# A block-sparse attention and MLP kernel: another order of a batch's tiles, and other sources for the first tiles' V

## The chip, the core and the metric

The kernel runs on one core of a Trainium2 chip. Its engines run side by side, each through its own list of instructions: PE (matmul), PEld (its weight loads), DVE and ACT (vector and scalar work), POOL (GpSimd), and SP, which here only issues DMAs. POOL issues DMAs too, through a queue of its own. The metric is the time of one execution in microseconds (us), lower is better.

## The reference

Attention with a mask of blocks, then a two-layer MLP on its output, in fp32.

```python
batch, n_heads, seq, head_dim = (4, 8, 768, 64)      # blocks of 32: 24 block rows, 3 sampled blocks a row
mask = np.abs(blk_i - blk_j) <= window               # window = 1
mask = mask | (blk_i == 0) | (blk_j == 0) | (blk_i == n_blocks - 1) | (blk_j == n_blocks - 1)
mask[qb * block:(qb + 1) * block, kb * block:(kb + 1) * block] = True   # for kb in sampled_blocks[qb]
scores = np.where(mask, scale * q @ k.T, -1e9)
attn = softmax(scores)
x = (attn @ v)                                       # 3072 tokens x 512
h = np.maximum(x @ w_in, 0.0)                        # 512 x 2048
out = h * h @ w_out                                  # 2048 x 512
```

So each query block sees its neighbours, the first and the last block (static, the same for all), and three sampled ones. The first and the last block row of a batch see all keys.

## The kernel before

**Tiles and chunks.** A tile is 128 rows (four query blocks) of a batch with all eight heads; a batch has NT = 6. Three tiles (UC) make a chunk of 384 tokens, so there are NCH = 8 chunks, two of a batch. A tile is done in two Halves of four heads: scores s (L374), maxima m (L385), exps p (L423), turn pt (L437) and its copies pT (L446), values pv (L459), norm rec and x (L474 to L479). The global rows, first and last block of a batch, are done by four Wholes, a head pair each: g (L546), exps pg (L562), turn ptg (L584), copies pTg (L592, L594), pvg (L604), norm. They fill the first rows of tile 0 and the last rows of tile 5. A Whole reads its V from vn, a batch's V rows (L222, two halves of 780 KB, one buffer for each half); a Half reads V, which is put together from static blocks (L203 and copies L209), neighbours (the window, L304, or copies L217 out of vn) and sampled blocks (L317, 12 loads a tile). Keys of a tile stand in KG: static (L284), sampled (copies L263 by POOL out of kn in batch 0, DMAs L276 later); neighbours are read from kn itself.

**The MLP.** For a chunk, moe() turns x (xt, L773, with the casts xh and xl, L776 and L777), makes ph for each of 16 slices of 128 hidden units (L788), r and g out of it (L792 to L806), and po (L816 in chunk 0, L826 later). In matmuls, values are split in a high and a low part. The weights come as 64-bit floats (craw, L692, on POOL's queue); cut() makes fp32 of them in chunk 0: two ACT passes (L708, L710) and two DVE passes (L719, L720); high and low parts follow (L726, L727, L752, L755).

**The order of work.** It is written out by hand: each engine runs in the order in which the program records. A Stream steps through units and resumes each after lags set by tables (LAG_0 and so on). Chunk 0's units run before any MLP work; that stretch is called the startup here. While moe(c) runs, the units of chunk c + 1 are recorded between its steps. Before the change a batch's Wholes stand in the even chunks, so batch 0's are in the startup, and the order of tiles is 0 to 5. In the loop of the startup, copies of static blocks and windows and cuts are put in at set steps (FIXED_0, MOVES_0, CUT_0). On PSUM a pool of five banks goes round among s, pt, g, xt and ph.

Of the kernel before, what the change touches and what calls it, by code (L numbers as in the profile page):

```python
# [2 lines left out]

# [66 lines left out]

STEP_0 = 5
STEP_1, FIRST_1 = 12, 0
LAG_1 = {**LAG, "v": 10, "x": 3, "t": 6, "v0": 5, "n": 0}
LAG_0 = {"s": 2, "x": 2, "t": 3, "c": 2, "v0": 2, "n": 2}
# [4 lines left out]
MOVES_0 = 22


FIXED_0 = 7
ON_ACT = 12
KEYS_N = 2
# [12 lines left out]
def tile_block_sparse_attention_moe(ctx: ExitStack, tc, kd, knd, qd, qgd, vd, vnd, samp, const, wcat, out):  # L97
# [112 lines left out]

    def copy_window(k, i, j, n, copy):

        b, t = order[k]
        blk = centre(NJ * t + j) - 1 + n
        assert 0 < blk < NBLK - 1
        r = blk % NJ * BLK
        copy(V[k][1][(1 + n) * BLK : (2 + n) * BLK, i, j], st["vn", b, i][r : r + BLK, blk // NJ])  # L217

    def load_vn(b, hf, eng=nc.sync, own=None):

        vn = (own or rot).tile([P, NT, HW // 2], F32, tag="vn", name=f"vn{b}_{hf}", bufs=1)
        eng.dma_start(vn.rearrange("p t c -> p (t c)"), vnd[b, hf])  # L222
# [30 lines left out]
    def copy_keys(b, t, own=None):  # L253

        vals = sampled(t, 0, POOL)
        kg = keys_of(b, t, own)
        for u in range(2):
            if t < UC:
                static_keys(b, t, u, nc.gpsimd.tensor_copy)
            kn = st["kn", b, u]  # L260
            for j in range(NJ):
                for r in range(NRAND):
                    nc.gpsimd.tensor_copy(  # L263
                        kg[:, j, 2 + r, 2 * u : 2 * u + 2].unsqueeze(1), kn[:, bass.ds(vals[NRAND * j + r], 1)]
                    )
                yield
# [13 lines left out]
    def static_keys(b, t, u, copy=nc.scalar.copy):  # L280

        src = st["kn", b, u][:, 0 : NBLK : NBLK - 1].rearrange("p i a c -> p i (a c)").unsqueeze(1)
        dst = st["kg", b, t][:, :, 0:2, 2 * u : 2 * u + 2].rearrange("p j i a c -> p j i (a c)")
        copy(dst, src.broadcast_to(list(dst.shape)))  # L284
# [480 lines left out]
    def turn(c):  # L765

        xh = pool["x"].tile([P, NCC, TOK], F32R, tag="xh", name=f"xh{c}", bufs=1)
        xl = pool["x"].tile([P, NCC, TOK], F32R, tag="xl", name=f"xl{c}", bufs=1)
        for i in range(UC):
            x = X.pop(order[c * UC + i])  # L770
            pt = bank(f"xt{c}_{i}")
            for cc in range(NCC):
                nc.tensor.transpose(pt[:, cc * P : (cc + 1) * P], x[:, cc * P : (cc + 1) * P], ident)  # L773
            p3 = pt.rearrange("p (c q) -> p c q", c=NCC)
            at = slice(i * P, (i + 1) * P)
            nc.scalar.copy(xh[:, :, at], p3)  # L776
            nc.vector.tensor_tensor(xl[:, :, at], p3, xh[:, :, at], op=ALU.subtract)  # L777
        xs[c] = (xh, xl)

# [115 lines left out]
    for k in range(2):  # L895
        deque(copy_keys(0, k), 0)
    for _ in range(AHEAD):
        cut_next()
    for k in range(1, UC):
        if k == 1:  # L900
            for f, *at in windows[k, 0]:
                f(*at, nc.gpsimd.tensor_copy)
            deque(copy_keys(0, 2, begin), 0)
# [102 lines left out]
```

## Time and profile before

| | us |
|---|---|
| median of 3 runs | 759.31 (759.08 to 762.59) |
| the profiled execution | 760.55, span 758.8 |
| PE busy in the span | 732.4 (97%) |
| ACT, POOL, DVE busy | 539.7, 502.3, 499.8 |
| first xt (x of chunk 0 is complete) | 57.3 |
| DMA, mean | 128 GB/s, 283 in the first 19 us |

The span is that of the profiled execution from its first to its last instruction; the time beside it includes what lies around. The rows of the trace are read as start, duration, engine, line, operation, output and inputs, count; in brackets stands how long the engine was idle before and what ended that. ph, po and s overlap their neighbours on PE, so that their price is the distance from start to start.

### The profile page before, as it was taken

To read this page: it belongs to the slowest core of one execution; us is meant where nothing else is said; L and a number is where in the kernel's file an instruction comes from. 1 tells how busy PE (TensorE), PEld (TensorE's weight loads), DVE (VectorE), ACT (ScalarE), POOL (GpSimd) and SP (SyncE) were. 2 spreads that over 40 slices of the span, in tenths; PEclk is the share of its full clock that TensorE was granted. 3 is DMA by queue.
4 is the path that set the end of the run, shared out by engine and by line. 5 is a ranking of instruction groups with operands and counts; after the bars stand their busy time and mean duration, and the time that the engine had idled before them with its cause. 6 is when DMAs were issued, how large, how long until landed. Compare 5 with 4: busy or idle time off the path is not lost.

```text
span 758.8 us, 26292 instructions
## 1 busy us (share of the span) xinstructions
PE 732.4 (97%) x9832; PEld 612.3 (81%) x9832; DVE 499.8 (66%) x987; ACT 539.7 (71%) x1193; POOL 502.3 (66%) x636
## 2 busy tenths in 40 slices
PE   4879999999999999999999999999999999999997
PEld 2656776668888888888888888887888888888986
DVE  5785785658785756667777575666868666645452
ACT  5896877798876876789786767679876776733222
POOL 6963844227776675757767567666876575777885
PEclk9799999999999999999999999999999999999999
DMA  8776799544543536544434344655344352201001
GB/s 283 224 215 172 228 264 344 130 117 131 140 114 93 146 86 176 153 109 128 113 105 106 101 126 109 221 120 140 79 124 118 75 143 64 51 1 44 1 1 41
DMA packets 92290, 97.45 MB, mean 128 GB/s; under 512 B 14787, under 2 KB 79428, under 8 KB 92164
## 3 DMA queue, kind: packets, MB, share of 16 engines
q1 hardware_dynamic: 86036, 72.41, 37.1%
q0 software_dynamic: 5696, 22.58, 9.2%
q8 instruction: 78, 1.28, 0.7%
q10 hardware_dynamic: 432, 0.79, 0.3%
q14 instruction: 48, 0.39, 0.2%
HBM read 89.43 MB, written 6.29 MB: 126 GB/s over the span
## 4 chain that ended last, share of the span: by engine, by line
PE 85%; ACT 5%; DMA 4%; DVE 4%; issue 1%; SPq 1%; ACTq 0%; POOL 0%; DVEq 0%; POOLq 0%
PE ph L788 33%; PE po L826 30%; PE s L374 7%; PE pv L459 5%; PE po L816 4%; PE g L546 2%; PE pvg L604 2%; DMA V<-in_v_dram 2%; DMA KG<-in_k_dram 1%; PE xt L773 1%; PE pt L437 1%; DVE xl L777 1%; ACT V L209 1%; DMA kn<-in_kn_dram 1%; SPq L317 1%
## 5 line engine op out<-in xcount | busy, mean ns | idle before, releaser
L413 ACT ACTIVATE pm<-p 32x256 f32<-32x256 f32 x576 | 239.2, 415 | 13.2 <-DVE p L391 4.8
L788 PE MATMUL ph<-xh,wi 128*128 128x384 f32 x832 | 237.8, 347 | 0.0
L826 PE MATMUL po<-wo,gh 128*128 128x512 f32 x672 | 213.8, 399 | 0.0
L755 POOL TENSOR_TENSOR wi<-W,wi 128x512 fp32r<-128x512 f32 x104 | 142.3, 1368 | 68.4 <-DVE wi L754 35.2
L806 POOL TENSOR_TENSOR gl<-gf,gh 128x384 fp32r<-128x384 f32 x112 | 117.4, 1048 | 93.0 <-DVE gf L804 80.6
L755 POOL TENSOR_TENSOR wo<-WO,wo 128x512 fp32r<-128x512 f32 x112 | 145.9, 1302 | 49.5 <-DVE wo L754 48.5
L792 ACT ACTIVATE r<-ph 128x384 f32<-128x384 f32 x128 | 63.0, 492 | 161.3 <-PE ph L788 156.1
L804 DVE SCALAR_TENSOR_TENSOR gf<-ph,r 128x384 f32<-128x384 f32 x112 | 62.3, 556 | 150.3 <-ACT r L792 136.4
L788 PEld LDWEIGHTS ph<-xh,wi 128*128 128x128 f32 x832 | 150.4, 188 | 13.4 <-issue 7.4
L826 PEld LDWEIGHTS po<-wo,gh 128*128 128x128 f32 x672 | 123.5, 188 | 23.0 <-issue 2.8
L788 PE MATMUL ph<-xl,wi 128*128 128x384 f32 x416 | 141.4, 340 | 0.0
L826 PE MATMUL po<-wo,gl 128*128 128x512 f32 x336 | 133.2, 396 | 0.0
L754 DVE CAST wo<-WO 128x512 fp32r<-128x512 f32 x112 | 84.4, 753 | 0.0
L788 PEld LDWEIGHTS ph<-xl,wi 128*128 128x128 f32 x416 | 78.2, 188 | 6.9 <-issue 2.9
L826 PEld LDWEIGHTS po<-wo,gl 128*128 128x128 f32 x336 | 63.1, 188 | 15.7 <-POOL gl L806 1.0
L385 DVE TENSOR_REDUCE m<-s 128x2 f32<-128x512 f32 x96 | 61.6, 683 | 11.2 <-PE s L374 10.9
L799 ACT ACTIVATE gh<-r 128x384 fp32r<-128x384 f32 x112 | 59.0, 526 | 9.3 <-ACT r L792 0.4
L459 PEld LDWEIGHTS pv<-V,pT 128*32 128x32 f32 x3072 | 47.7, 110 | 19.8 <-issue 9.5
L459 PE MATMUL pv<-V,pT 128*32 128x65 f32 x3072 | 56.2, 223 | 5.0 <-ACT pT L446 4.8
L788 PE MATMUL ph<-xh,WI 128*128 128x384 f32 x192 | 54.4, 344 | 0.8 <-ACT xh L776 0.8
L374 PE MATMUL s<-KG,q 64*32 64x160 f32 x1536 | 51.2, 305 | 1.4 <-issue 1.0
L418 DVE STREAM_TRANSPOSE pT<-pm 128x1024 f32<-128x1024 f32 x36 | 44.6, 1239 | 4.9 <-ACT pm L413 4.7
(85 smaller groups left out, 933.0 us busy)
## 6 DMA issues: line engine op xcount, KB each, us to landing
craw<-in_w_dram POOLq DMA_DIRECT2D x32, 512.0 KB, 5.9
V<-in_v_dram SPq DMA_DIRECT2D x504, 32.5 KB, 1.8
KG<-in_k_dram SPq DMA_DIRECT2D x216, 64.0 KB, 2.0
V<-in_v_dram SPq DMA_DIRECT2D x28, 390.0 KB, 4.5
q<-in_q_dram SPq DMA_DIRECT2D x24, 256.0 KB, 3.0
out_dram<-ot SPq DMA_DIRECT2D x21, 256.0 KB, 2.5
V<-in_v_dram SPq DMA_DIRECT2D x16, 292.5 KB, 4.2
vn<-in_vn_dram SPq DMA_DIRECT2D x5, 780.0 KB, 6.4
```

The costliest lines, as they stand in the source:

```text
L374: nc.tensor.matmul(self.sb[e][j * BLK : (j + 1) * BLK, i * NSLOT + a : i * NSLOT + z], q[r, j, pr, :], k, start=True, stop=True,)
L385: nc.vector.tensor_reduce(m[:, e], self.sb[e].rearrange("p (i c) -> p i c", i=2), axis=AX, op=ALU.max)
L413: nc.scalar.activation(p[a * BLK : (a + 1) * BLK, j], x[j * BLK : (j + 1) * BLK, :, a], AF.Exp, scale=SCALE)
L459: nc.tensor.matmul(po[j * BLK : (j + 1) * BLK, h * VW : (h + 1) * VW], self.pT[:, j, 2 * e + i, c], v[:, self.u, j, hv : hv + VW], start=( ...
L754: nc.vector.tensor_copy(w[:, 0], src)
L755: nc.gpsimd.tensor_tensor(w[:, 1], src, w[:, 0], op=ALU.subtract)
L788: nc.tensor.matmul(ph[:, :TOK], w, x, start=(i == 0), stop=(i == len(steps) - 1))
L792: nc.scalar.activation(r, ph[:, :TOK], AF.Relu)
L799: nc.scalar.activation(gh, r, AF.Square)
L804: nc.vector.scalar_tensor_tensor(gf, ph[:, :TOK], 0.0, r, op0=ALU.max, op1=ALU.mult)
L806: nc.gpsimd.tensor_tensor(gl, gf, gh, op=ALU.subtract)
L826: nc.tensor.matmul(acc[c][u], g[:, at], w[:, k], start=(f == 0 and i == 0), stop=(f == NF - 1 and i == 2))
```

## The change

A batch's tiles are taken in the order 1 to 5, 0. Chunk 2b then holds tiles 1 to 3 of batch b, and chunk 2b + 1 tiles 4, 5, 0, and the Wholes run beside that second chunk: those of batch 0 while moe(0) runs, those of batch b while moe(2b) runs. V's windows of the second and third tile come from memory by POOL's queue (copy_window goes; there were 48 such copies, 12 on POOL, 18 on DVE, 18 on ACT by the table); vn of batch 0 is loaded later, on SP. Keys' static copies of the first three tiles go from POOL to ACT, V's static copies from ACT to DVE. x of chunk 0 is turned tile by tile in the startup and not in one go at moe(0)'s start. Lags and steps of the tables are set anew (EARLY 23 to 21, STEP_0 5 to 4, LAG_0, LAG_1, WO_LOW 3 to 2). The counts of matmuls stay.

```diff
-CUT_0 = (30, 5)
+CUT_0 = (13, 7)
-order = [(b, t) for b in range(B) for t in range(NT)]
+order = [(b, t % NT) for b in range(B) for t in range(1, NT + 1)]
 def copy_keys(b, t, own=None):
-            if t < UC:
-                static_keys(b, t, u, nc.gpsimd.tensor_copy)
+            if k < UC:
+                static_keys(b, t, u)
...
 def units(c):
-        wholes = [] if c % 2 else [Whole(c // 2, pr) for pr in range(NPAIR)]
+        wholes = [] if c % 2 == 0 else [Whole(c // 2, pr) for pr in range(NPAIR)]
...
         if c == 1:
-            return [(i * STEP_1 + FIRST_1, u) for i, u in enumerate(halves)]
+            both = [(i * STEP_1 + FIRST_1, u) for i, u in enumerate(halves)]
+            both += [(i * STEP_1 + FIRST_1 + G_1, u) for i, u in enumerate(wholes)]
+            return sorted(both, key=lambda x: x[0])
...
 def moe(c):
-        if c < NCH:
+        if 0 < c < NCH:
             turn(c)
...
 # the startup
     load_keys(0, 0, nc.gpsimd)
-    load_whole(0)
-    load_q(0, 0)
+    load_keys(0, 1, nc.gpsimd)
+    load_q(*order[0])
+    load_window(0, 0)
     load_static(0, 0)
-    load_vn(0, 0, nc.gpsimd)
-    load_keys(0, 1, nc.gpsimd)
-    load_vn(0, 1, nc.gpsimd, begin)
-    load_window(0, 0)
-    load_q(0, 1)
     load_sampled(0, 0, nc.sync, SP)
-    load_sampled(1, 0, nc.sync, SP)
-    load_q(0, 2, own=begin)
-    load_sampled(2, 1, nc.sync, SP)
-    windows = {
-        (k, u): [(copy_window, k, u, j, n) for j in range(NJ) for n in range(3)] for k in range(1, UC) for u in range(2)
-    }
...
+    load_q(*order[1], nc.gpsimd)
+    load_q(*order[2], nc.gpsimd, "x", 5)
+    others = [
+        lambda: load_window(1, 0, nc.gpsimd),
+        lambda: load_sampled(1, 0, nc.sync, SP),
+        lambda: load_window(2, 1, nc.gpsimd),
+        lambda: load_sampled(2, 1, nc.sync, SP),
+        lambda: load_whole(0),
+        lambda: load_vn(0, 0),
+    ]
+    for i, _ in enumerate(chain(copy_keys(*order[0]), copy_keys(*order[1]), copy_keys(*order[2], begin))):
+        for at, f in chain(zip(LOADS_0, [cut_next] * AHEAD), zip(OTHERS_0, others)):
+            if at == i:
+                f()
     fixed = [(copy_static, k, i) for k in range(UC) for i in range(2)]
...
+    turns = [(2 * STEP_0 * i + STEP_0 + TURN_0[0], i) for i in range(UC)]
     for at, u in units(0):
+        while turns and turns[0][0] < at:
+            turn_at, i = turns.pop(0)
+            work.add(turn_at, 0, lambda i=i: turn_tile(0, i, TURN_0[1]))
         work.add(at, 0, lambda u=u: u.run(side, LAG_0))
...
         if now >= FIXED_0 and fixed:
             f, *at = fixed.pop(0)
-            f(*at, nc.scalar.copy)
-        if now >= MOVES_0 and moves:
-            f, *at = moves.pop(0)
             f(*at, nc.vector.tensor_copy)
```

Three places in the order. The first is SP at the start: the names are q (queries by batch and tile), V0 and V1 (the first tile's V), V10 and V11, V20 and V21 (the second's and third's); idx are the sampled numbers. Before:

```order
L170 DMA QG_77<-in_qg_dram 128x512
L242 DMA q0_0_129<-in_q_dram 128x512
L203 DMA V0_78<-in_v_dram 64x260 x2
L304 DMA V1_79<-in_v_dram 96x260 x2
L304 DMA V1_79<-in_v_dram 96x3x260 [waits DMAHW0_49]
L304 DMA V1_79<-in_v_dram 96x3x260 [waits DMAHW1_49]
L242 DMA q0_1_143<-in_q_dram 128x512 [waits DMAHW2_49]
L231 TENSOR_LOAD idx_116 [waits DVE_49]
L317 DMA V0_78<-in_v_dram 32x2x260 [waits DMAHW3_49]
L317 DMA V0_78<-in_v_dram 32x2x260 [waits DMAHW4_49]
L317 DMA V1_79<-in_v_dram 32x2x260 [waits DMAHW5_49]
```

and now:

```order
L238 DMA q0_1_132<-in_q_dram 128x512
L302 DMA V1_79<-in_v_dram 96x4x260 x2
L207 DMA V0_78<-in_v_dram 64x260 x2
L227 TENSOR_LOAD idx_115 [waits DVE_49]
L315 DMA V0_78<-in_v_dram 32x2x260
L315 DMA V0_78<-in_v_dram 32x2x260 [waits DMAHW0_49]
L315 DMA V1_79<-in_v_dram 32x2x260 [waits DMAHW1_49]
L315 DMA V0_78<-in_v_dram 32x2x260 [waits DMAHW2_49]
```

QG and the second and third q are gone from here, and the sampled loads start right behind the first tile's window; each waits for a semaphore in turn, eight in all. POOL's queue at the start, where kn are the keys of the two head halves and the copies are sampled keys; before:

```order
L175 DMA kn_0_126<-in_kn_dram 128x1536
L222 DMA vn_0_133<-in_vn_dram 128x1560
masks.py:199 AFFINE_SELECT ident<-ident 128x128
L175 DMA kn_1_135<-in_kn_dram 128x1536
L222 DMA vn_1_137<-in_vn_dram 128x1560
L231 TENSOR_LOAD idx
L284 COPY KG_93<-kn_0_126 128x4x2x64
L263 COPY KG_93<-kn_0_126 128x64
```

and now:

```order
L179 DMA kn_0_128<-in_kn_dram 128x1536
L179 DMA kn_1_130<-in_kn_dram 128x1536
masks.py:199 AFFINE_SELECT ident<-ident 128x128
L238 DMA q_2_175<-in_q_dram 128x512
L238 DMA q_3_177<-in_q_dram 128x512
L227 TENSOR_LOAD idx
L260 COPY KG_93<-kn_0_128 128x64
```

The queue has both kn and two q where vn stood; weights (craw) and the four windows are issued between the key copies that follow. The second place is ACT at the start of moe(0), from gp0_0 to r0_1 (the numbers are chunk and slice; ct, WO and W are weights being cut; p are exps). Before:

```order
L792 ACTIVATE r0_0_1570<-ph0_0_1518 128x384
L795 ACTIVATE gp0_0_1572<-r0_0_1570 128x384
L708 ACTIVATE ct4_1574<-craw4_0_982 128x512
L710 ACTIVATE craw4_0_982<-craw4_0_982,below_75 128x512
L752 CAST wi0_2_1581<-W12_81 128x512
L423 ACTIVATE p0_3_0_1564<-s0_3_0_0_1523,m0_3_0_1561 128x256 x2
L423 ACTIVATE p0_3_0_1564<-s0_3_0_1_1524,m0_3_0_1561 128x256 x2
L792 ACTIVATE r0_1_1601<-ph0_1_1584 128x384
```

and now:

```order
L800 ACTIVATE r0_0_1279<-ph0_0_1226 128x384
L803 ACTIVATE gp0_0_1281<-r0_0_1279 128x384
L710 ACTIVATE WO0_95<-craw0_1_358 128x512
L712 ACTIVATE craw0_1_358<-craw0_1_358,below_75 128x512
L754 CAST wi0_2_1297<-W12_81 128x512
L710 ACTIVATE WO1_96<-craw1_1_724 128x512
L712 ACTIVATE craw1_1_724<-craw1_1_724,below_75 128x512
L710 ACTIVATE ct4_1306<-craw4_0_932 128x512
L712 ACTIVATE craw4_0_932<-craw4_0_932,below_75 128x512
L423 ACTIVATE p0_4_0_1295<-s0_4_0_0_1241,m0_4_0_1292 128x256 x2
L423 ACTIVATE p0_4_0_1295<-s0_4_0_1_1242,m0_4_0_1292 128x256 x2
L800 ACTIVATE r0_1_1333<-ph0_1_1313 128x384
```

Two more cuts (WO0, WO1) stand between. The third place is SP at the switch from batch 1 to 2. Before:

```order
L317 DMA V1_79<-in_v_dram 32x260 [waits DMAHW0_49]
L175 DMA kn2_0_5572<-in_kn_dram 128x1536 [waits DMASW7_49,DMAHW1_49,DMASW0_49,PE_49]
L170 DMA QG_77<-in_qg_dram 128x512 [waits DMAHW2_49,DMASW0_49]
L222 DMA vn2_0_5575<-in_vn_dram 128x1560 [waits DMAHW3_49]
L304 DMA V1_79<-in_v_dram 96x3x260 [waits DMAHW4_49,PE_49]
L304 DMA V1_79<-in_v_dram 96x260 [waits DMAHW5_49,PE_49]
L231 TENSOR_LOAD idx_116
```

and now:

```order
L315 DMA V1_79<-in_v_dram 32x260 [waits DMAHW0_49]
L179 DMA kn2_0_5461<-in_kn_dram 128x1536 [waits DMASW3_49,DMAHW1_49,DMASW0_49,PE_49]
L174 DMA QG_77<-in_qg_dram 128x512 [waits DMAHW2_49,DMASW4_49]
L218 DMA vn2_0_5464<-in_vn_dram 128x1560 [waits DMAHW3_49,PE_49]
L302 DMA V1_79<-in_v_dram 96x260 [waits DMAHW4_49]
L302 DMA V1_79<-in_v_dram 96x3x260 [waits DMAHW5_49]
L227 TENSOR_LOAD idx_115
```

vn2_0 now waits for PE too (the last pvg of batch 1), and the loads of V, kn, q and KG follow it on the queue.

More of the change, by code (lines that the diff above doesn't have):

```diff
@@ L2 @@
 from contextlib import ExitStack, suppress
+from itertools import chain
 import numpy as np
@@ L64 @@
 STEP = PIECES // (2 * UC)
-EARLY = 23
+EARLY = 21
 LAST = 4
@@ L69 @@
 G_AT = 9
[L71 to L74, printed above, removed]
-CUT_0 = (30, 5)
+STEP_0 = 4
+STEP_1, FIRST_1 = 12, 2
+G_1 = 4
+TURN_0 = (16, 1)
+LOADS_0 = (0, 1, 4, 8, 12)
+OTHERS_0 = (3, 4, 5, 6, 16, 16)
+LAG_1 = {**LAG, "v": 10, "x": 2, "t": 7, "v0": 5, "n": 0}
+LAG_0 = {"s": 1, "x": 2, "t": 2, "c": 1, "v0": 6, "n": 1}
+CUT_0 = (13, 7)
 CUT_1 = 3
[L79 to L84, printed above, removed]
+FIXED_0 = 2
+KEYS_N = 3
 MOVED = 6
-WO_LOW = 3
+WO_LOW = 2
 PLAIN = 16
@@ L209, in copy_static, with load_vn @@
         copy(dst, src.broadcast_to(list(dst.shape)))
[L211 to L221, printed above, removed]
+    def load_vn(b, hf, eng=nc.sync):
+        vn = rot.tile([P, NT, HW // 2], F32, tag="vn", name=f"vn{b}_{hf}", bufs=1)
         eng.dma_start(vn.rearrange("p t c -> p (t c)"), vnd[b, hf])
@@ L237, in sampled, with load_q @@
         )[1]
-    def load_q(b, t, eng=nc.sync, own=None):
-        q = (own or rot).tile([P, NJ, NPAIR, BLK], F32, tag="q", name=f"q{b}_{t}", bufs=1 if own else 2)
+    def load_q(b, t, eng=nc.sync, tag="q", bufs=2):
+        q = rot.tile([P, NJ, NPAIR, BLK], F32, tag=tag, name=f"q{b}_{t}", bufs=bufs)
         n = NJ * NPAIR * BLK
@@ L361, in scores @@
             q, kg, kn = st["q", b, t], st["kg", b, t], st["kn", b, u]
+            assert b == 0 or t not in (1, 2) or st["fixed", b, t, u]
             self.sb = [bank(f"s{self.name}_{e}") for e in range(2)]
@@ L398, in next_keys @@
         def next_keys(self):
-            b, t = order[min(self.k + self.u, len(order) - 1)]
-            if b > 0 and t < 2:
+            k = min(self.k + self.u, len(order) - 1)
+            b, t = order[k]
+            if b > 0 and k % NT < 2:
                 static_keys(b, t, 1 - self.u)
@@ L483, in loads @@
             k = order.index((self.b, self.t))
-            if step == 0 and self.t == NT - 1 and self.b + 1 < B:
+            if step == 0 and self.t == order[-1][1] and self.b + 1 < B:
                 eng = nc.gpsimd if self.b == 0 else nc.sync
@@ L501, in loads @@
             if step == 2 and k not in range(1, UC) and n < len(order):
-                if self.t == NT - 1:
+                if self.t == order[-1][1]:
                     load_static(n, self.u)
@@ L533, in run @@
             po = self.values(bank)
-            if self.pr == 1 and self.b > 0:
+            if self.pr == 1:
                 load_vn(self.b, 1)
@@ L765, in turn, with turn_tile @@
     def turn(c):
-        xh = pool["x"].tile([P, NCC, TOK], F32R, tag="xh", name=f"xh{c}", bufs=1)
-        xl = pool["x"].tile([P, NCC, TOK], F32R, tag="xl", name=f"xl{c}", bufs=1)
         for i in range(UC):
[L770 to L778, printed above, removed]
+            deque(turn_tile(c, i), 0)
+    def turn_tile(c, i, lag=0):
+        if i == 0:
+            xs[c] = [
+                pool["xs"].tile([P, NCC, TOK], F32R, tag=tag, name=f"{tag}{c}", bufs=1) for tag in ("xh", "xl")
+            ]
+        xh, xl = xs[c]
+        x = X.pop(order[c * UC + i])
+        pt = bank(f"xt{c}_{i}")
+        for cc in range(NCC):
+            nc.tensor.transpose(pt[:, cc * P : (cc + 1) * P], x[:, cc * P : (cc + 1) * P], ident)
+        yield lag
+        p3 = pt.rearrange("p (c q) -> p c q", c=NCC)
+        at = slice(i * P, (i + 1) * P)
+        nc.scalar.copy(xh[:, :, at], p3)
+        nc.vector.tensor_tensor(xl[:, :, at], p3, xh[:, :, at], op=ALU.subtract)
     def hidden(c, f):
@@ L837, in emit_out @@
                 nc.scalar.copy(o, acc[c][u])
-            r0 = (c * UC + u) * P
+            b, t = order[c * UC + u]
+            r0 = (b * NT + t) * P
             (nc.scalar if c == NCH - 1 else nc.sync).dma_start(out[r0 : r0 + P, :], o)
@@ L874, in tile_block_sparse_attention_moe @@
     st["idx"] = indices()
+    pool["xs"] = ctx.enter_context(tc.tile_pool(name="xs", bufs=1, reuse_waits="tile"))
     start = tc.tile_pool(name="start", bufs=1)
@@ L879, in tile_block_sparse_attention_moe @@
     load_keys(0, 0, nc.gpsimd)
-    load_whole(0)
-    load_q(0, 0)
+    load_keys(0, 1, nc.gpsimd)
+    load_q(*order[0])
+    load_window(0, 0)
     load_static(0, 0)
-    load_vn(0, 0, nc.gpsimd)
-    load_keys(0, 1, nc.gpsimd)
-    load_vn(0, 1, nc.gpsimd, begin)
-    load_window(0, 0)
-    load_q(0, 1)
-    load_sampled(0, 0, nc.sync, SP)
-    load_sampled(1, 0, nc.sync, SP)
-    load_q(0, 2, own=begin)
-    load_sampled(2, 1, nc.sync, SP)
-    windows = {
-        (k, u): [(copy_window, k, u, j, n) for j in range(NJ) for n in range(3)] for k in range(1, UC) for u in range(2)
-    }
[L895 to L903, printed above, removed]
+    load_sampled(0, 0, nc.sync, SP)
+    load_q(*order[1], nc.gpsimd)
[7 more added lines that the diff above has]
+        lambda: load_vn(0, 0),
+    ]
+    for i, _ in enumerate(chain(copy_keys(*order[0]), copy_keys(*order[1]), copy_keys(*order[2], begin))):
+        for at, f in chain(zip(LOADS_0, [cut_next] * AHEAD), zip(OTHERS_0, others)):
+            if at == i:
+                f()
     fixed = [(copy_static, k, i) for k in range(UC) for i in range(2)]
-    fixed += windows[2, 0] + windows[2, 1][:ON_ACT]
-    moves = windows[1, 1] + windows[2, 1][ON_ACT:]
     side = lambda name: ps_o.tile([P, 512], F32, tag="o", name=name)
     work = Stream()
+    turns = [(2 * STEP_0 * i + STEP_0 + TURN_0[0], i) for i in range(UC)]
     for at, u in units(0):
+        while turns and turns[0][0] < at:
+            turn_at, i = turns.pop(0)
+            work.add(turn_at, 0, lambda i=i: turn_tile(0, i, TURN_0[1]))
         work.add(at, 0, lambda u=u: u.run(side, LAG_0))
+    for turn_at, i in turns:
+        work.add(turn_at, 0, lambda i=i: turn_tile(0, i, TURN_0[1]))
     now = 0
```

2 lines of the change are left out of this document (added).

## Prediction

> **What bounds the kernel now.** I read the engines' busy shares first, then the span cut into stretches, then the rows at the seams of those stretches, and the queue that brings V last.
>
> ```profile
> PE 732.4 (97%) x9832; PEld 612.3 (81%) x9832; DVE 499.8 (66%) x987; ACT 539.7 (71%) x1193; POOL 502.3 (66%) x636
> ```
>
> PE is busy 97% of the span. The stretches (start:end, length, then busy time and count of PE, PEld, DVE, ACT, POOL, then granted clock, DMA share, GB/s) say where the other 26 us are:
>
> ```profile
> 20.00:30.00 10.00, 7.80 (x270) 6.12 (x261) 7.53 (x24) 9.72 (x24) 9.44 (x26) 0.84 0.94 300
> ...
> 345.00:754.00 409.00, 408.20 (x4980) 354.76 (x4966) 263.69 (x506) 269.02 (x612) 290.64 (x279) 1.00 0.35 90
> ```
>
> From 345 us to the tail PE misses 0.8 us in 409. In the stretch at 20 it waits 2.2 of 10, while ACT is full (9.7) and the DMA engines are 0.94 busy. So the time is the startup, then PE's work, then whatever stalls a new order brings into the full stretch. Moving work between the two is worth what it takes off the startup, less what it adds to PE's stretch.
>
> The seam, on PE (start, duration, line, operation, shapes, count, idle before):
>
> ```profile
> 56.03 1.38 PE L459 MATMUL pv<-V,pT 128*32 128x65 f32 x64 [0.97 <-ACT pT L446]
> 57.34 1.53 PE L773 MATMUL xt<-ident,x 128*128 128x128 f32 x12
> 59.64 0.44 PE L788 MATMUL ph<-xh,WI 128*128 128x384 f32 x1 [0.78 <-ACT xh L776]
> ...
> 61.30 0.40 PE L374 MATMUL s<-kn,q 64*32 64x96 f32 x16
> ...
> 62.44 0.44 PE L788 MATMUL ph<-xl,WI 128*128 128x384 f32 x1
> ```
>
> From 62.44 ph flows. Ahead of it stand 1.14 of s (61.30 to 62.44) and four ph, about 0.7, that belong to the full stretch already. So the startup is worth 62.44 - 1.14 - 0.7 = 60.6 us.
>
> **The change: what PE takes over.** The four wholes of batch 0 (g, ptg, pvg) leave the startup and come into chunk 0, where PE has no gap for them. Price of one:
>
> ```profile
> 15.24 0.88 PE L584 MATMUL ptg<-ident,pg 128*128 128x128 f32 x6
> 15.96 1.46 PE L546 MATMUL g<-kn,QG 128*128 128x512 f32 x4
> ...
> 24.01 0.89 PE L604 MATMUL pvg<-vn,pTg 128*32 128x65 f32 x48
> 24.83 0.87 PE L584 MATMUL ptg<-ident,pg 128*128 128x128 f32 x6
> ```
>
> From start to start 0.72 (15.24 to 15.96) and 0.82 (24.01 to 24.83), and 1.46 for g: 3.0, and 12.0 for four. The other batches' twelve wholes only go one stage later, from one full stage to another: nothing on PE. The break-even is a startup of 60.6 - 12.0 = 48.6 us.
>
> **The new startup.** ACT, full before, loses much there: the window copies, the static copies, the wholes' exps and turns, and two of the six cuts in the loop. It gets the static keys. What remains, from the rows of one half and one cut:
>
> ```profile
> 43.84 1.07 ACT L446 COPY pT<-pt 128x512 f32<-128x512 f32 x2
> 44.80 1.58 ACT L423 ACTIVATE p<-s,m 128x256 f32<-128x256 f32 x4
> 46.23 0.70 ACT L708 ACTIVATE W<-craw 128x512 f32<-128x512 f32 x1
> ...
> 58.03 1.56 ACT L776 CAST xh<-xt 128x512 fp32r<-128x512 f32 x3 [0.29 <-PE xt L773]
> ```
>
> and on POOL:
>
> ```profile
> 6.62 0.61 POOL L284 COPY KG<-kn 128x512 f32<-128x512 f32 x1 [2.65 <-DMA kn<-in_kn_dram]
> 7.17 2.17 POOL L263 COPY KG<-kn 128x64 f32 x12
> ...
> 36.23 0.53 POOL L692 DMA_DIRECT2D craw<-in_w_dram  x1
> ```
>
> Six halves of 2.65, four cuts of 1.40 (this and a second pass of 0.75, in a row further down), two casts of 0.6, xh 1.56 and six static keys at POOL's 0.61 make 15.9 + 5.6 + 1.2 + 1.6 + 3.7 = 28.0 us. From 6.6, when the keys land, and with some 5 us in which ACT can't start (12 key copies and the first half's s and maxima come first: 2.17, 1.14 and, an estimate, 1.5), that ends near 39.5; with the last half's pv, norm and turn behind it, near 44. POOL's 72 key copies at 0.18 and nine DMA issues at 0.53 are 17.8, so they end near 24.4. Neither is what ends last. V is:
>
> ```profile
> 8.21 25.50 SPq L317 DMA_DIRECT2D V<-in_v_dram  x24
> ...
> 35.36 10.22 SPq L317 DMA_DIRECT2D V<-in_v_dram  x12
> ...
> 48.46 6.62 SPq L317 DMA_DIRECT2D V<-in_v_dram  x12
> ```
>
> These are the 36 sampled loads of the first three tiles, and 12 of the next. The same issue takes 1.06 us while POOL's queue moves vn and the DMA engines are 0.94 busy, 0.85 behind it, 0.55 with short transfers alone. Each waits on SP for the load eight places before it (the order shows the eight semaphores in turn), so the pace is the landing over eight, or the issue's own 0.55. The change leaves them on SP, back to back, from about 7.3. Beside them POOL's queue now brings both keys, two q, five craw and, where vn stood, the two windows: 4 times 390 KB, as much as the two vn of 780. So the first 24 go at 1.06 again, to 32.8, and the last 12 at 0.85, to 43.0. Least, median and longest time to landing in the first two stretches (20 to 34, 35 to 46):
>
> ```profile
> DMA to landing us min/median/max: 2.3/6.1/8.3
> ...
> DMA to landing us min/median/max: 2.2/3.6/5.4
> ```
>
> Second tile's V at about 36.8 (I take 4.0 for the landing, between the median of its stretch and the least), third at 46.6. Behind the third stand two pv of 1.38, and norm, xt, xh and xl, which took 3.18 at the seam above (the last pv's end at 57.41 to the ph at 60.59 that waited for xl): 5.9, so 52.5. Behind the second stand, in the new order of PE and ACT, a pv, a pt (1.16, as 8/6 of the ptg's 0.87), three pairs of copies, two of exps, three cuts, a cast and three xh: 1.38 + 1.16 + 3.21 + 3.16 + 4.2 + 0.6 + 1.56 = 15.3, so 52.1. Rows of ACT overlap the next by 0.1 (43.84 and 1.07, against 44.80), so a dozen joins take 1.2 off the second chain; between 50.9 and 52.5 I take 51.5: **+2.9**. Bounds: 0.55 for every load puts V out of the way, and the 44 above holds, -4.6; 1.06 for all 36 (45.5) and the 3.6 and 5.9 give 55.0, +6.4.
>
> **x turned tile by tile, windows without copies, static V on DVE.** The turn takes two of three xt, xh and xl off the end of the startup; it is in the 5.9 and the 15.3. The 48 window copies go, their price is part of ACT's relief. Static V on DVE (six) costs nothing while DVE waits for s; bounds 0 and, as ACT's rows below have it, 0.84 to 0.99 each. What DVE does to POOL beside it has a row:
>
> ```profile
> 11.36 2.53 ACT L209 COPY V<-V 64x780 f32<-64x780 f32 x3
> 15.21 2.98 ACT L209 COPY V<-V 64x1040 f32<-64x1040 f32 x3
> ...
> 28.48 2.49 POOL L263 COPY KG<-kn 128x64 f32 x12
> ```
>
> The last ran beside DVE's window copies, 0.32 longer than the 2.17 above: little. [...]
>
> **Chunk 0's first steps.** Only four cuts are made before the MoE, not six. Two more stand on ACT between gp0_0 and r0_1:
>
> ```profile
> 65.16 0.65 ACT L708 ACTIVATE ct<-craw 128x512 f32<-128x512 f32 x1
> 65.71 0.75 ACT L710 ACTIVATE craw<-craw,below 128x512 int32<-128x512 uint16 x1
> 66.36 0.60 ACT L752 CAST wi<-W 128x512 fp32r<-128x512 f32 x1
> ...
> 344.48 0.31 PE L374 MATMUL s<-kn,q 64*32 64x96 f32 x7 [0.75 <-ACT pg L562]
> ```
>
> Each is 1.20 from start to start: r0_1 comes 2.4 us later, and the wholes' exps stand in the same queue. PE has other work meanwhile, until it wants a bank that ACT has not read. Bounds 0 and 5 (the two cuts and four pg exps of 0.5); the nearest price of a late ACT in a full stage is the 0.75 at 344.48. Two of these: **+1.5**. Little can be gained, since PE hardly waits in this stretch before.
>
> **The batch switches.** A batch's wholes now end just before the next batch, and they read vn. On SP vn2_0 waits for PE's last pvg of batch 1, with the next tile's V, kn, q, KG and the next V queued behind it. Before, from vn to the last of those V loads:
>
> ```profile
> 297.65 0.42 SPq L222 DMA_DIRECT2D vn<-in_vn_dram  x1
> ...
> 300.89 9.34 SPq L317 DMA_DIRECT2D V<-in_v_dram  x12
> ...
> 312.23 7.28 SPq L276 DMA_DIRECT2D KG<-in_k_dram  x12
> ...
> 322.33 7.33 SPq L317 DMA_DIRECT2D V<-in_v_dram  x12
> ```
>
> and on PE:
>
> ```profile
> 338.04 0.63 PE L826 MATMUL po<-wo,gh 128*128 128x512 f32 x2
> ...
> 338.74 0.63 PE L826 MATMUL po<-wo,gh 128*128 128x512 f32 x2
> ...
> 340.14 0.34 PE L788 MATMUL ph<-xh,WI 128*128 128x384 f32 x1
> ...
> 342.07 0.33 PE L788 MATMUL ph<-xh,WI 128*128 128x384 f32 x1
> 342.33 1.12 PE L459 MATMUL pv<-V,pT 128*32 128x65 f32 x64
> ```
>
> 297.65 to 329.66 and a landing of 2.2 (the least above) are 34.2 us, which ends 10.5 us ahead of the pv at 342.33: no stall. A po takes 0.23 there (three in 0.70, 338.04 to 338.74), a ph 0.175 (eleven in 1.93, 340.14 to 342.07). In the new order 68 ph, 51 po, two halves' s and pv, three xt and a pvg lie between that pvg and the pv of the second tile: 11.9 + 11.9 + 2.3 + 2.2 + 1.5 + 0.8 = 30.6 us. So 34.2 would stall PE for 3.6, at both such switches (batches 1 to 2 and 2 to 3). If the 12 loads of 9.34 go like those of 7.33, it is 1.6; with some of the issues at the 0.55 seen above, nothing. I take 0.9 each, between 0 and 1.6: **+1.8**, bounds 0 and 7.2 (no gain, since there was no stall to lose). Batch 0 to 1 goes by POOL's queue with little behind it: nothing.
>
> **Sum.** The profiled execution took 760.55 (span 758.8), 1.24 over the median of 759.31. 760.55 + 2.9 + 1.5 + 1.8 = 766.75, and against the median **765.5**, 0.8% slower.
>
> **Rivals.**
> A, not slower: the sampled loads run faster than 1.06, since the windows on POOL's queue go out in shorter rows than vn's and the long craw transfers are spread between key copies. At 0.55 to 0.7 V is in by 36, and ACT's chain ends the startup at 44: -4.6 in place of +2.9, 758.0. It decides below a startup of 45.3, where the 3.3 of the later waits are paid. If PE rides over those too, 754.7. For it: 0.55 alone; against it: a DMA share of 0.94 at 300 GB/s, with no fewer bytes to move.
> B: the startup as forecast, and PE rides over the later waits as it does before: 760.55 + 2.9 - 1.24 = 762.2.
> C: DVE's copies hold POOL: six of up to 0.99 keep its queue filled 5.9 us longer, and 5.9 / 1.06 = 5.6 more loads cost 1.06 and not 0.55: +2.8, 768.3. Against it: 0.32 in twelve copies. [...]
> D: the switches at their full 3.6: 7.2 in place of 1.8, 770.9. For it: that is the queue's pace as it stands in the rows.
>
> **Chances.** Forecast 0.36, A 0.28, B 0.14, C 0.10, D 0.12. Half a per cent is about what can be told from no change. Of A 0.17 ends below 755.5 and 0.11 above it; B is 0.13 within the half per cent and 0.01 above; the rest is above 763.1. Faster 0.17, same 0.24, slower 0.59. The range takes in A with PE riding over its stalls and D with some of C: 754.5 to 772, under 2 in 10 outside. The forecast's own range is 763 to 768.
>
> **What would show it.** Right: PE's first flowing ph near 51 or 52, with pv of the third tile waiting for V by SP's loads at 1 us each; ACT with gaps in the startup; idle PE of 0.5 to 1 us near the first r of chunk 0; SP's vn of batches 2 and 3 released by PE's pvg and a short PE wait at the pv behind it. Wrong: sampled loads at 0.7 or less, V in by 38, and ph flowing before 47; or PE's stretch after the startup without gaps, in which case only the startup's difference is left.

## The result

The changed kernel is slower: 769.10 us (median of four runs, 768.45 to 772.55) against 759.63 (759.08 to 762.59) in the same comparison, a ratio of 1.0126 with a 95% interval of 1.0086 to 1.0166. The profiled execution took 768.45 with a span of 766.7, 7.9 more than the span of before.

The page of the changed kernel and its stretches (start:end, length, busy time and count of PE, PEld, DVE, ACT, POOL, then granted clock, DMA share, GB/s):

```profile
PE 735.5 (96%) x9832; PEld 612.0 (80%) x9832; DVE 509.9 (67%) x981; ACT 526.3 (69%) x1169; POOL 495.3 (65%) x622
...
20.00:30.00 10.00, 6.52 (x117) 4.77 (x118) 3.63 (x6) 2.64 (x6) 7.31 (x31) 0.52 1.05 259
30.00:40.00 10.00, 7.54 (x290) 6.05 (x292) 7.40 (x17) 6.88 (x15) 10.00 (x51) 1.00 0.63 167
...
345.00:754.00 409.00, 408.12 (x5049) 353.84 (x5048) 268.52 (x513) 273.38 (x625) 292.93 (x286) 1.00 0.37 95
```

ACT, full at 20 us before, is now busy 2.64 of 10 there; the startup is no longer ACT's. PE is still full from 65 us on (67.49 busy of 68 to 133 us, 212.00 of 212 to 345, then the third stretch above). The seams on PE show where the 7.9 us come from. Changed kernel, rows as in the prediction:

```profile
48.32 1.29 PE L459 MATMUL pv<-V,pT 128*32 128x65 f32 x64
...
52.77 0.44 PE L781 MATMUL xt<-ident,x 128*128 128x128 f32 x2 [1.16 <-DVE x L479]
53.89 0.45 PE L796 MATMUL ph<-xh,WI 128*128 128x384 f32 x1 [0.68 <-ACT xh L785]
54.79 0.45 PE L796 MATMUL ph<-xl,WI 128*128 128x384 f32 x1 [0.46 <-DVE xl L786]
...
162.60 1.47 PE L781 MATMUL xt<-ident,x 128*128 128x128 f32 x12
...
762.10 0.39 PE L834 MATMUL po<-wo,gl 128*128 128x512 f32 x1
```

and the anchors of before that the prediction did not show, with the one long wait of that stretch:

```profile
133.42 0.33 PE L374 MATMUL s<-KG,q 64*32 64x160 f32 x2 [1.04 <-issue]
...
157.36 1.47 PE L773 MATMUL xt<-ident,x 128*128 128x128 f32 x12
...
754.21 0.40 PE L826 MATMUL po<-wo,gl 128*128 128x512 f32 x1
```

I count the startup to the first ph that reads xl, less one ph ahead of it (0.18), which gives 60.4 before (60.59) and 54.6 now (54.79). From there to chunk 1's xt it is 97.0 before and 108.0 now; from that xt to the last po 596.9 and 599.5. So the startup gives 5.8 us, chunk 0's stretch takes 11.0, and the rest takes 2.6.

Three groups of rows answer to the steps of the prediction. SP, POOL and the PE rows that wait for POOL in the startup, changed kernel:

```profile
6.24 38.02 SPq L315 DMA_DIRECT2D V<-in_v_dram  x36
...
10.25 0.71 POOL L302 DMA_DIRECT2D V<-in_v_dram  x1
15.51 0.70 POOL L302 DMA_DIRECT2D V<-in_v_dram  x1 [4.55 <-issue]
...
22.17 0.68 POOL L302 DMA_DIRECT2D V<-in_v_dram  x1 [2.14 <-issue]
...
28.98 8.57 POOL L260 COPY KG<-kn 128x64 f32 x48
...
16.84 0.74 PE L373 MATMUL s<-KG,q 64*32 64x160 f32 x4 [4.57 <-POOL KG L260]
...
23.48 1.00 PE L373 MATMUL s<-KG,q 64*32 64x160 f32 x6 [3.82 <-POOL KG L260]
...
39.80 1.11 PE L459 MATMUL pv<-V,pT 128*32 128x65 f32 x64
```

The 36 sampled loads go at 1.06 each to 44.3. POOL stands before its windows for 4.55, 0.47 and 2.14 (7.2 in all), with key copies queued behind them, and makes the 72nd of them, the last of the third tile, near 34.9 (33rd of the 48 in the last POOL row). The scores of the first tile's second half wait for these copies (4.57, 1.34 and 3.82), the last of them until 23.48. The row at 39.80 is the second tile's first pv: its V had landed at 35.6, and it does not wait for it. Nor does the third tile's first pv (48.32 above; its V landed at 46.4). PE's pauses in the startup:

```profile
35.01 1.11 PE L459 MATMUL pv<-V,pT 128*32 128x65 f32 x63 [1.12 <-issue]
...
38.88 0.98 PE L437 MATMUL pt<-ident,p 128*128 128x128 f32 x7 [1.33 <-issue]
...
43.76 0.49 PE L373 MATMUL s<-KG,q 64*32 64x160 f32 x10 [1.78 <-issue]
```

Each stands inside a group (63 of 64 pv, 7 of 8 pt, 10 of 64 s), and no semaphore ended it: 4.2 us. And chunk 0 and the first switch:

```profile
63.24 2.81 PE L824 MATMUL po<-WO,gp 128*128 128x512 f32 x6 [1.49 <-DVE WO L722]
...
71.26 0.67 PE L373 MATMUL s<-kn,q 64*32 64x96 f32 x9 [0.50 <-ACT pg L562]
...
376.62 1.37 PE L459 MATMUL pv<-V,pT 128*32 128x65 f32 x58 [0.59 <-DMA V<-in_v_dram]
```

A correction to the kernel's description: by the rows of before the 48 window copies were 24 on ACT, 12 on DVE and 12 on POOL, not 18, 18 and 12.

### The profile page after: what moved, and what is told of

The parts are those of the page before. It is cut to its first block, busy times and chain, and to the rows that moved or that the text cites. A ratio compares the mean times of both kernels' runs of the same rounds, so it can differ in the third digit from the quotient of the medians.

```text
span 766.7 us, 26249 instructions
## 1 busy us (share of the span) xinstructions
PE 735.5 (96%) x9832; PEld 612.0 (80%) x9832; DVE 509.9 (67%) x981; ACT 526.3 (69%) x1169; POOL 495.3 (65%) x622
## 3 DMA queue, kind: packets, MB, share of 16 engines
q1 hardware_dynamic: 86036, 73.48, 36.8%
## 4 chain that ended last, share of the span: by engine, by line
PE 88%; SPq 4%; issue 3%; ACT 1%; DVE 1%; POOL 1%; DMA 1%; POOLq 0%; ACTq 0%
PE ph L796 34%; PE po L834 29%; PE s L373 7%; PE pv L459 6%; PE po L824 5%; PE g L546 3%; SPq L315 2%; PE pvg L604 2%; PE pt L437 1%; PE xt L781 1%; SPq L273 1%; POOL KG L260 1%; SPq L227 0%; DMA V<-in_v_dram 0%; PE ptg L584 0%
## 5 line engine op out<-in xcount | busy, mean ns | idle before, releaser
L757 POOL TENSOR_TENSOR wo<-WO,wo 128x512 fp32r<-128x512 f32 x112 | 145.1, 1296 | 56.8 <-DVE wo L756 54.4
L373 PE MATMUL s<-KG,q 64*32 64x160 f32 x1536 | 56.6, 311 | 12.5 <-POOL KG L260 10.4
L459 PEld LDWEIGHTS pv<-V,pT 128*32 128x32 f32 x3072 | 46.4, 109 | 16.7 <-issue 11.8
L756 DVE CAST wi<-W 128x512 fp32r<-128x512 f32 x91 | 52.4, 575 | 0.0
## 6 DMA issues: line engine op xcount, KB each, us to landing
V<-in_v_dram SPq DMA_DIRECT2D x504, 32.5 KB, 1.9
```

The costliest lines, as they stand in the source:

```text
L373: nc.tensor.matmul(self.sb[e][j * BLK : (j + 1) * BLK, i * NSLOT + a : i * NSLOT + z], q[r, j, pr, :], k, start=True, stop=True,)
L459: nc.tensor.matmul(po[j * BLK : (j + 1) * BLK, h * VW : (h + 1) * VW], self.pT[:, j, 2 * e + i, c], v[:, self.u, j, hv : hv + VW], start=( ...
L756: nc.vector.tensor_copy(w[:, 0], src)
L757: nc.gpsimd.tensor_tensor(w[:, 1], src, w[:, 0], op=ALU.subtract)
```

## The experiments

The questions were what sets the new startup, what the moved wholes cost, and what the later 2.6 us are. A startup's length can't be read closer than about 2 us: three kernels with the same program up to its end (the changed one, and the fifth and sixth below) have 54.6, 57.0 and 55.5. Part of this is PE's granted clock, which is below 1.00 at places that differ from one execution to the next. The changed kernel, the fifth variant and the sixth (granted clock third from the end):

```profile
40.00:50.00 10.00, 8.10 (x280) 6.32 (x270) 5.43 (x15) 8.33 (x19) 1.23 (x7) 1.00 0.89 280
50.00:60.00 10.00, 7.71 (x157) 6.25 (x156) 8.06 (x14) 5.27 (x11) 8.83 (x23) 1.00 0.88 228
...
40.00:50.00 10.00, 6.84 (x204) 5.72 (x192) 3.40 (x10) 6.02 (x15) 1.02 (x5) 0.83 0.98 302
...
40.00:50.00 10.00, 7.67 (x212) 6.33 (x203) 4.76 (x13) 6.96 (x16) 1.82 (x8) 0.83 0.92 299
50.00:60.00 10.00, 7.70 (x175) 5.66 (x164) 7.25 (x13) 4.54 (x8) 8.28 (x23) 0.75 0.81 226
```

From the end of PE's third pause to the end of the startup it is 10.8 in the changed kernel, and 12.0 and 11.9 in the two others. The sixth variant's stretch from there to chunk 1's xt is 110.6 and not 108.0, with the same program: from the ph that reads xl to the first po it takes 11.06 (55.66 to 66.72), and 8.45 in the changed kernel (54.79 to 63.24), which is the whole difference. Ratios are to the kernel before, with 95% intervals. Lines of the variants differ by a few numbers.

### Room in POOL's queue

```diff
-dynamic_dma_scratch_size=1024
+dynamic_dma_scratch_size=1920
```

> The changed kernel with 1,920 bytes a partition for the descriptors of POOL's DMA queue, not 1,024; nothing else. Theory R (POOL's key copies stand behind the windows' DMAs, and these wait for room in the queue's descriptors): POOL's idle 7.2 us ahead of L302 falls below 2, the second half's scores end near 18 and not 25, and the startup (54.6) shortens by 2 to 6 us. Theory V (the sampled loads on SP set the end): the idle may go, but the startup shortens by under 1.5, since the last of the 36 is still issued near 44. Theory L (DVE's static copies lock POOL out): the idle before L302 stays within 1 us of 7.2, and the time within 1 us.

771.57 us, 1.0154 (1.0096 to 1.0211). POOL in this kernel, before the last of the four windows:

```profile
15.39 0.68 POOL L302 DMA_DIRECT2D V<-in_v_dram  x1 [1.75 <-issue]
...
23.10 8.53 POOL L260 COPY KG<-kn 128x64 f32 x48
...
29.05 0.40 PE L459 MATMUL pv<-V,pT 128*32 128x65 f32 x2 [4.08 <-DMA V<-in_v_dram]
```

The idle falls from 7.2 to 1.75, the key copies come 5.9 us earlier (23.10 against 28.98), and the startup is 56.2, not shorter. With the windows sent earlier the 36 sampled loads take 42.0 and not 38.0, PE waits 3.5 for the keys of the first tile's second half in place of 9.7, but 8.9 for the first tile's V (four waits, the longest above), and the third tile's V lands at 49.9 in place of 46.4. So the room is what POOL waits for, and once it is there V comes later. What the wait for room costs with V unchanged is not shown.

### The windows on SP

```diff
-        lambda: load_window(1, 0, nc.gpsimd),
+        lambda: load_window(1, 0),
...
-        lambda: load_window(2, 1, nc.gpsimd),
+        lambda: load_window(2, 1),
```

> The changed kernel with the four windows of the second and third tile issued on SP, ahead of those tiles' sampled loads, not on POOL. Theory R: POOL has no idle before its key copies, the second half's scores end near 15 and the startup shortens by 2 to 6 us, unless V becomes later. Theory V: the last sampled load is issued 1 to 3 us later than 44.3, and the startup is unchanged or up to 3 longer. Theory L: as before, within 1 us.

769.33 us, 1.0131 (1.0074 to 1.0188). POOL has no idle at the windows, and the startup is 55.8. The last sampled loads, 12 from 38.43 for 9.36 us, end 3.5 later than 44.3, a little beyond the 1 to 3 expected, and the third tile's V lands at 49.4. That is Theory V's case, with an end within the spread of the startups. Here and in the first variant 6.3 us lie between that landing and the end, near the forecast's 5.9; in the changed kernel it is 8.2.

### V's static copies back on ACT

```diff
-            f(*at, nc.vector.tensor_copy)
+            f(*at, nc.scalar.copy)
```

> The changed kernel with V's static copies on ACT, as in the kernel before, not on DVE. Theory L: POOL's idle before L302 (7.2) and its slow key copies shrink, and the startup shortens by 2 or more. Theories R and V: no change of POOL's idle within 0.5, startup within 1 us.

772.48 us, 1.016 (1.0103 to 1.0217). POOL without DVE's copies beside it:

```profile
15.62 0.70 POOL L302 DMA_DIRECT2D V<-in_v_dram  x1 [4.80 <-issue]
...
22.19 0.68 POOL L302 DMA_DIRECT2D V<-in_v_dram  x1 [1.94 <-issue]
```

With a third wait of 0.75 between these it is 7.5 in all, against 7.2: the same idle without the copies. POOL's key copies keep their pace too (45 in 8.01, against 48 in 8.57). DVE isn't what holds POOL here. The startup is 56.9, at the end of the spread and not below it.

### More cuts in the startup

```diff
-CUT_0 = (13, 7)
+CUT_0 = (13, 4)
```

> The changed kernel with a cut every 4 steps of the startup's loop and not every 7 (CUT_0 (13, 4)): more cuts on ACT before the MLP, where ACT idles, and fewer between gp0_0 and r0_1. If chunk 0's late start comes from those cuts: PE's idle of 1.49 before po (L824) at 63.24 and of 0.50 at 71.26 go, 1 to 2 us off the whole, the startup itself within 1.5 longer. Rival: the startup takes back what the cuts cost, and the time is the same within 0.5.

771.55 us, 1.0158 (1.0102 to 1.0215). PE's 1.49 and 0.50 are gone, and from the first ph to chunk 1's xt it is 107.0, 1.0 less. A slower stretch hides part of it: from the ph that reads xl to the first g PE takes 6.7 here and 5.5 in the changed kernel, with the same matmuls (mean granted clock of the execution 0.988 against 0.991); without these 1.2 it would be 2.2 less, by my estimate. The startup is 56.8: its last xt waits 2.63 for DVE's x in place of 1.16, and its pauses are 5.1 in place of 4.2. That the two waits come from those cuts is shown. The whole time is no shorter, as the rival has it, though not within its 0.5.

### Without batch 0's wholes

```diff
+            if b == 0 and t in (0, NT - 1):
+                nc.vector.memset(X[b, t][0:BLK] if t == 0 else X[b, t][P - BLK : P], 0.0)
...
-        wholes = [] if c % 2 == 0 else [Whole(c // 2, pr) for pr in range(NPAIR)]
+        wholes = [] if c % 2 == 0 or c == 1 else [Whole(c // 2, pr) for pr in range(NPAIR)]
```

> The changed kernel without the four wholes of batch 0 (their rows of x are set to zero, so that part of the attention is left out). Theory P (the moved work costs what it takes on PE, since PE is full beside chunk 0): from the first flowing ph to chunk 1's xt 11 to 13.5 us less than the 108.0 of the changed kernel, and the time 1.5% less. Rival G (the wholes fill gaps that PE has there anyway): under 8 us less.

761.63 us, 1.0013 (0.9985 to 1.0040). PE:

```profile
57.20 0.44 PE L798 MATMUL ph<-xl,WI 128*128 128x384 f32 x1 [0.37 <-DVE xl L788]
...
65.61 4.51 PE L826 MATMUL po<-WO,gp 128*128 128x512 f32 x6 [2.76 <-DVE WO L724]
69.56 0.74 PE L798 MATMUL ph<-xh,wi 128*128 128x384 f32 x1
...
155.23 1.47 PE L783 MATMUL xt<-ident,x 128*128 128x128 f32 x12
```

From 57.0 (57.20 less 0.18) to 155.23 it is 98.2, 9.8 less than with the wholes. But the six po behind the wait take 3.95 here from start to start (65.61 to 69.56), at a lower granted clock (0.97 on average from 65 to 133 us, 1.00 in the changed kernel), and 2.25 in the changed kernel (63.24 to 65.49). Without these 1.7 it is 11.5 less, and 12.3 if the longer wait is taken off too (2.76 where the changed kernel waits 1.49 and 0.50). That is in Theory P's range: the wholes find next to no gap on PE. The span falls by 6.6 alone (766.7 to 760.1), as this startup was 2.4 longer and the rest 0.7; the median falls by 7.5, 1.0% where 1.5% was expected.

### vn behind V on SP

```diff
                 if self.u == 0:
                     load_whole(self.b + 1, eng)
-                    load_vn(self.b + 1, 0, eng)
+                    if self.b == 0:
+                        load_vn(self.b + 1, 0, eng)
...
+            if step == 2 and 0 < self.b < B and order.index((self.b, self.t)) % NT == 0 and self.u == 1:
+                load_vn(self.b, 0) if self.b > 1 else None
```

> The changed kernel with the first vn half of batches 2 and 3 loaded on SP behind the next batch's first tile's V, kn and q, so that nothing queued there waits for the last pvg. If the switch's wait comes from that queue: PE's wait at pv near 376 (0.6, with slow pv rows 1.1) goes, and the time falls by 0.5 to 1.1; by the forecast's term it would be 1.8. Rival: the wait stays, since V's own loads are what is late, and the time is the same within 0.5.

770.10 us, 1.0107 (1.0051 to 1.0163): by the whole time no difference from the changed kernel that can be told. By the trace there is one:

```profile
166.06 1.47 PE L784 MATMUL xt<-ident,x 128*128 128x128 f32 x12
...
378.89 1.11 PE L459 MATMUL pv<-V,pT 128*32 128x65 f32 x64
...
763.55 0.39 PE L837 MATMUL po<-wo,gl 128*128 128x512 f32 x1
```

The same pv now runs without a wait, and from chunk 1's xt to the last po it is 597.5, against 599.5; the eight other variants of the changed kernel have 599.0 to 600.4. In the profiled execution the 2.6 of chunk 0 at a lower clock hide it. The 2.0 us lie in the one stage with the switch from batch 1 to 2 (chunk 3's xt to chunk 4's: 84.1 against 86.2; 84.4 to 87.1 in the others); the stage of the switch from 2 to 3 has 84.1 and 84.2. That this queue holds PE fits. But three other variants (the fifth, the eighth and the last) show no wait at this pv either, without the edit, so that one execution doesn't say how much of the 2.0 the edit gives.

### craw later

```diff
-LOADS_0 = (0, 1, 4, 8, 12)
+LOADS_0 = (0, 1, 20, 22, 23)
```

> The changed kernel with three of the five first craw loads behind the third tile's key copies (LOADS_0 (0, 1, 20, 22, 23)). Theory V (DMA bandwidth and the pace of V's loads set the startup): the third tile's V lands 2 to 4 us before 46.4, PE's pauses inside a group of matmuls (1.1, 1.3 and 1.8) get shorter, and the startup falls from 54.6 to 51 to 53. Rival K (the chain of work behind sets it): V lands earlier, the startup stays within 1 us, or is longer because a cut waits for its craw.

770.30 us, 1.0126 (1.0068 to 1.0184). Both theories miss. The second tile's V lands 1.4 earlier (34.2), the third's 1.3 later (47.7): the three craw now move at 32 to 47, beside the last sampled loads, where the DMA share is 1.04. PE's pauses are 0.56, 1.88 and 1.62, and a fourth of 1.58 stands in a pv at 52.02. Startup 57.3. So here a transfer moved within the startup displaced another.

### The third tile's loads on ACT

```diff
-        lambda: load_sampled(2, 1, nc.sync, SP),
+        lambda: load_sampled(2, 1, nc.scalar, mybir.EngineType.Activation),
```

> The changed kernel with the third tile's 12 sampled loads issued by ACT, beside SP's, in the time in which ACT idles (15 to 26 us). Theory Q (SP's queue sets V's pace, each load waiting for the one eight before): the third tile's V lands before 36, and the second's stays at 35.6 within 2. Theory B (the DMA engines are full and the pace is shared): the second tile's V lands 4 or more later than 35.6, the last of both near 44 again. The startup falls by 1 to 3 in the first case and by nothing in the second.

782.38 us, 1.0272 (1.0218 to 1.0326). SP's and ACT's queues, and PE:

```profile
6.24 37.44 SPq L315 DMA_DIRECT2D V<-in_v_dram  x24
...
10.85 23.23 ACTq L315 DMA_DIRECT2D V<-in_v_dram  x12
...
36.72 1.97 PE L437 MATMUL pt<-ident,p 128*128 128x128 f32 x8 [11.04 <-ACT p L423]
```

With two queues, SP's 24 loads take 1.56 each and ACT's 12 take 1.94; all 36 are issued by 43.7, as from one queue by 44.3. So the pace isn't that of SP's queue: a load takes 1.04 over both queues together (36 in 37.4 us) and 1.06 from one (38.0), at a DMA share of 1.07 and 1.06 in the two stretches from 10 to 30 us and 0.64 from 30 to 40 (1.07, 1.05 and 0.63 in the changed kernel). That fits Theory B; that the DMA engines are what the two share is my reading. The second tile's V lands at 49.1, not at 35.6. The 13 us more are another matter, which I hadn't thought of: in ACT's order the exps stand behind its loads, which end at 34.08, and PE waits 11.04 for them.

### Parts of the change in the kernel before

The third tile's windows from memory, on POOL's queue, in the kernel before; and then the second's too:

```diff
+    load_window(2, 1, nc.gpsimd)
...
-    fixed += windows[2, 0] + windows[2, 1][:ON_ACT]
```

> The kernel before with one part of the change alone: the third tile's windows come from memory (two DMAs on POOL's queue behind the five craw) and ACT's 24 window copies go; order of tiles, wholes and the rest stay. Theory A (before, ACT's work set the startup: 24 copies are 9.7 us): the startup falls from 60.4 to 53 to 57, the whole time by 3 to 7 us. Theory D (V's landing or PE's own chain is close behind): the startup falls by under 2.

> The kernel before with the windows of the second and the third tile from memory (four DMAs on POOL's queue behind the five craw), so no window copies on POOL, ACT and DVE. Theory A: as with the third tile alone or up to 2 us better. Theory D: 1.56 MB more on full DMA engines, some 5 us: the third tile's V lands at 50 or later and not at 48.2, and the startup is no shorter than with the third tile alone, or longer by up to 3.

With one tile's windows 760.45 us, 1.0016 (0.9991 to 1.0042), with both 761.43, 1.0027 (0.9999 to 1.0055): no gain. The first of the two:

```profile
20.00:30.00 10.00, 6.51 (x241) 5.00 (x239) 8.60 (x29) 3.68 (x9) 3.52 (x8) 1.00 0.91 295
...
30.91 0.71 POOL L304 DMA_DIRECT2D V<-in_v_dram  x1 [5.70 <-issue]
...
51.53 0.98 PE L459 MATMUL pv<-V,pT 128*32 128x65 f32 x50 [0.41 <-DMA V<-in_v_dram]
...
58.72 0.45 PE L788 MATMUL ph<-xl,WI 128*128 128x384 f32 x1 [0.51 <-DVE xl L777]
```

ACT falls from 9.72 to 3.68 of 10 at 20 us, yet the startup falls by 1.9 alone (58.5), 0.7 with both (59.7), neither more than a startup differs from one execution to the next. POOL waits 5.70 ahead of its window, and the third tile's V lands at 51.5, 3.3 later than before, so that PE waits for it; with both it lands at 49.8. Before, ACT was full without being what alone set the end; V's transfers stood close behind it.

### Where PE pauses

```diff
-            for i in range(2):
+            for i in (0, 1, 0, 1) if self.k == 0 and u == 0 else (0, 1):
```

> The changed kernel with the scores of its first half made twice over (64 matmuls more, the same values), at 7 to 12 us, where PE waits for keys anyway. Theory I (PE's pauses inside a group of matmuls are its instruction stream coming in pieces of 128 matmuls with their loads): the pauses behind 1 of 64 pv, 1 of 8 pt and 54 of 64 s move 64 matmuls ahead, into groups where there was none, with 0.8 to 3 us each, and the startup is within 2 us of 54.6 to 57. Rival W (PE waits there for data, V or keys): the pauses stay at the same instructions.

772.88 us, one run. PE:

```profile
34.10 0.28 PE L373 MATMUL s<-kn,q 64*32 64x96 f32 x3 [0.96 <-issue]
...
37.92 0.32 PE L373 MATMUL s<-kn,q 64*32 64x96 f32 x8 [0.43 <-issue]
...
41.54 0.41 PE L459 MATMUL pv<-V,pT 128*32 128x65 f32 x10 [0.47 <-issue]
...
45.60 0.55 PE L459 MATMUL pv<-V,pT 128*32 128x65 f32 x24 [0.35 <-issue]
...
52.48 1.31 PE L459 MATMUL pv<-V,pT 128*32 128x65 f32 x39 [2.25 <-issue]
```

The pauses left their places (1 of 64 pv, 1 of 8 pt, 54 of 64 s) and stand inside s, s and pv. The second and third are 64 matmuls ahead to the one: 1 pt and 63 s back is the place behind 1 s (37.22 in the trace), 54 s and 10 pv back is the place behind 54 pv: Theory I. In the changed kernel they stand 128 and 125 matmuls apart (63 pv, 64 s and 1 pt; 7 pt, 64 pv and 54 s), and with their loads that is 250 to 256 instructions. Here all five are 125 or 126 apart. The DMA view of the changed kernel, cut at the pauses, has one packet of the instruction queue in 32 to 34 us, and one each in 36 to 38 and 40.5 to 43:

```profile
q8 instruction: 1, 0.02, 3.8%
...
q8 instruction: 1, 0.02, 4.4%
```

and none in the stretches between (34 to 36, 38 to 40.5). Place and packet fit Theory I; what such a packet brings is not shown. The pauses did not shrink: three are below the 0.8 that I expected, but all five are 4.5 us, against 4.2 in the changed kernel. The startup was 56.7, with V at 48.1.

## Why the prediction was right, and where it was off

It forecast 765.5 with 754.5 to 772: slower, by 0.8%, and it came out at 769.1, 1.26%. Against the profiled execution its sum was +6.2, and +7.9 was measured. Step by step:

- **The sum**: the startup came out 3.1 above its forecast, chunk 0's stretch 2.5 below, the rest 0.8 above. With 0.2 for the startup of before (60.4, not 60.6) these leave some 1.7, which is in part luck.
- **What bounds the kernel**: right. PE misses 0.9 us in 409 from 345 us on, and the time is the startup plus PE's work plus stalls.
- **The startup** (51.5): too short by 3.1. Its main step held well: the 36 loads at 1.06 to 44.3 (forecast 43.0), the second tile's V at 35.6 (36.8), the third's at 46.4 (46.6). What failed is the chain behind V: no pv of the second or third tile waits for V, and PE's own chain ends last. It began late, behind POOL's key copies (23.48), and came to the second tile's pv at 39.80, 4.2 after that V. It was also summed without PE's pauses at places of its instruction stream. Those of the changed kernel are 1.12 + 1.33 + 1.78 = 4.2; without them the startup would be 50.4, and in the fifth and sixth variants (6.0 and 4.7 us of pauses in 57.0 and 55.5) 51.0 and 50.8, of which 1.1 and 1.0 go to the lower clock. That the pauses are on the path there is argued from this difference; no run took them away alone, nor the late keys without a later V. The row was in the profile: before has one of 1.74 in its startup.
- **POOL's key copies "end near 24.4"**: wrong, 34.9. Windows were priced at 0.53 like the other DMAs; they cost 0.70 and 7.2 of waiting for room. Two variants that cut or removed the wait got no shorter startup, but both also got the third tile's V 3.0 to 3.5 later.
- **The wholes on PE** (12.0) and **chunk 0's first steps** (1.5): 13.5 forecast, 11.0 measured. Both prices held: at the same clock the fifth variant has 11.5 to 12.3 for the wholes, and the waits are 1.49 behind the late WO and 0.50 behind pg. What the sum left out is what this stretch of before held already: waits of 1.04 and 0.23, and one g of the next batch, which takes 1.21 from start to start (143.45 to 144.66).
- **The batch switches** (0.9 each): the sum is about right (2.6 in the rest of the kernel) and the place is not. The sixth variant is 2.0 shorter, all of it at batches 1 to 2.
- **Rival A** (V sooner) fell: with windows and craw moved, and with two queues, the 36 loads took 35.5 to 42.0 us. The 0.55 that spoke for it was misread: by the profile those 12 loads are of 32.5 KB each, where the 36 are of 65, and three craw were issued beside them (49.53, 51.16 and 54.35), so that no row here has the price beside short transfers alone. **Rival B** fell: the later waits are there. **Rival C** (DVE's copies hold POOL) fell: in the third variant POOL's idle is the same without them (7.5 against 7.2). No run shows the 2.8 that it was priced at; without those copies the startup came out at 56.9, not below 54.6. **D** was half right: one switch costs some 2.0 and not 3.6, the other nothing.
